# A fused attention-and-feed-forward kernel: a new written-out order on every engine, found with re-set transfer costs

## The chip, the cores and the metric

The kernel runs on one core of one Trainium2 chip. The core has a matrix engine (TensorE, PE in the profile, with its weight loads shown as PEld), three engines for elementwise work (VectorE is DVE, ScalarE is ACT, GpSimd is POOL) and SyncE (SP), which here issues nearly all DMA transfers. Every engine runs its own list of instructions strictly in order and waits at semaphores for what others have made. The metric is the device time of one execution in microseconds (us).

## The reference

```
phi(x)  = outer product of (S1 x) and (S2 x), 8 by 8 = 64 features    # x: 32 numbers per token and head
q_p, k_p = phi(q), phi(k)                  # q, k, v: 4 batches, 4 heads, 1088 tokens, 32 numbers
kv  = sum over tokens of k_p v             # 64 x 32 per batch and head
z   = sum over tokens of k_p
attn = (q_p kv) / (q_p z + 1e-6)
x   = attn with the heads side by side     # 4352 tokens of 128 numbers
h   = x @ w_in                             # 128 -> 2048
out = (h - tanh(h)) @ w_out                # 2048 -> 128, float32
```

## The kernel before

**Two halves that overlap.** The attention of a batch yields 1088 columns of `xT` (tokens along the free axis). The feed-forward walks over `xT` in ten windows (`layers`): two of 256 tokens, seven of 512, one of 256. A window `w` has sixteen first products `L1.w.j` (line 912, `w_in` times `xT` into a PSUM bank pair), tanh over up to four of them at once on ACT (line 916), and sixteen second products `L2.w.j` (line 925) that add up in bank 0. The term `h @ w_out` is done as one product with `w_in @ w_out`, which the kernel computes once: `turn0..3` transposes `w_in` on TensorE (line 857), `w_inT0..3` copies it (ACT, line 862), `wfold` multiplies (line 869), and `lin.w` (line 897) applies it. After the window, DVE copies bank 0 out (`osb`, line 931) and SP stores it (line 938).

**Attention of a batch b.** DVE transposes the loaded keys (`kT`, lines 569 and 573), TensorE projects (`kproj`, 582), DVE turns them (`kab`, 590), a small chain gives the weights for the denominator (`gram` 598, `zm` 603, `ufold` 606, `uw` 609). POOL and DVE form key products (`wk`, 629), and TensorE sums them with the values (`tiles` 642 for batch 0, `sums` 711 for the others; both need all four pieces of that batch's `v`). Queries: `qT` (739), `qproj` (751), `qab` (759), a divide chain (`dm` 778, `den`, `rden`, `qa` 787), query products `qp` (661 or 797), a transpose (`qt0` 676 with the copy `qpB` 683, or `qpT` 803), and the numerator `num` (693 or 820), whose result is copied into `xT` (`x`, 699, 830, 835). For batches 1 to 3 this stands between feed-forward products. Batch 0 has nothing to stand between: it is the opening, and the feed-forward starts behind it.

**What sets the order.** Each operation is recorded by `Program.op` with its engine, a cost and what it reads and writes. `schedule` places them. The list `ORDER` names for each engine the operations by number in the order in which they are to run; with it, the costs, rates and lags in the code no longer choose any order. What they still set is where TensorE's filler products (lines 503, 512 columns wide, and 504, 128 wide: products of zeros that keep the array busy in the opening) are put, because the scheduler fills the gaps that it computes. `sync` then derives every semaphore wait from the recorded dependences.

**Loads.** All go through SP's queue in the order of `ORDER["sync"]`: keys (`load_keys`, `load_rows`), queries (`load_rows`), values in four pieces per batch (`load_v`), `w_in` in four pieces `wi0..3` (`load_w_in`), `w_out` in four pieces `wo0..3` (`load_w_out`). `gated` adds a wait for an earlier load so that no more than about 2.4 MB are asked for ahead; the loads of batch 2 also wait for `x0.8` (the last copy of batch 0's numerators, DVE) and those of batch 3 for `x81.0` (the same of batch 1, ACT). SP waits at the instruction, so everything behind it in the queue waits as well. `w_in` and `w_out` are float32 in memory and are cast on chip: `cast_in0`, `cast_in1` on ACT, `cast_in2`, `cast_in3` and `cast_out0..3` on POOL (lines 843 and 847).

The one dependence that is touched is that of `psk0` and `psk1`, two small scaled copies on ACT (line 530), and the small operation `warm` (line 505, a tanh of one column, made ahead of need), which writes the tile `spare`.

Of the kernel before, what the change touches and what calls it, by code (L numbers as in the profile page):

```python
# [26 lines left out]
SEEN = {"tensor": 60, "scalar": 40, "vector": 50, "gpsimd": 70, "sync": 60}  # L27
MODE = 93
ISSUE = 460
BEGIN = 750  # L30
# [5 lines left out]

ORDER = {
    "tensor": (
# [14 lines left out]
    ),  # L53
    "scalar": (
# [4 lines left out]
    ),  # L59
    "vector": (  # L60
# [5 lines left out]
    ),  # L66
    "gpsimd": (
        "6 4 5 2 16 20 3 25 7 18 17 19 23 22 79 21 80 24 81 109 106 110 107 108 111 150 152 241 242 247 251 363 365 364 374 370 "
        "508 506 507 517 513 "
    ),  # L70
    "sync": (
# [3 lines left out]
    ),  # L75
}

# [16 lines left out]
class Program:  # L94
# [46 lines left out]
    def schedule(self):  # L141
# [7 lines left out]
            for x, i in enumerate(text.split()):  # L149
                turn[self.ops[int(i)]] = x  # L150
        head = dict.fromkeys(engines, 0)
        free = {e: 0 if e == "sync" else BEGIN for e in engines}
        avail = {e: [] for e in engines}
        for i, o in enumerate(self.ops):
            o.idx = i
# [7 lines left out]
        while left:  # L163
            best = None
            for e in engines:
# [4 lines left out]
                if turn:  # L170
                    o = min(avail[e], key=turn.get)
# [48 lines left out]
            order[e].append(o)  # L220
            left -= 1
            for k in o.kids:
                seen = o.end + SEEN[k.eng]
                if k.eng == e and not dma:
                    seen = o.at + o.cost if e == "tensor" else o.end
                k.ready = max(k.ready, seen)
                k.need -= 1
                if not k.need:
                    avail[k.eng].append(k)
# [114 lines left out]
def bass_polysketch_attn__then__act_tanh_shrink_kernel(nc, q, k, v, S1, S2, moe_w_in, moe_w_out, out):  # L344
# [92 lines left out]
    def load_small():  # L437
        for i, src in enumerate((S1, S2)):
            o = load("scalar", 1024, ("s_raw",), "s", -1000, lambda e, i=i, src=src: e.dma_start(
                out=s_raw[8 * i:8 * i + 8, :], in_=src[:, :]), True)  # L440
            o.lag = -950

    def cells(name, i, lo, hi):
        return [(name, i, c) for c in range(lo // 64, hi // 64)]
# [1 line left out]
    def load_rows(dst, src, name, b, cuts, prios, first=0):  # L446
        i = b % 2
        for x, (lo, hi) in enumerate(cuts):
            hi = min(hi, S)
            size = 512 * (hi - lo)  # L450
            o = P.op("sync", size / (360 if b else 280), lambda e, lo=lo, hi=hi: e.dma_start(
                out=dst[i][:, lo:hi], in_=src[b].rearrange("h (j c) d -> (h j) (c d)", j=32)[:, lo:hi]),
                w=cells(name + "raw", i, lo, hi), sem=f"{name}{i}{x + first}", prio=prios[x], name=f"load {name}{b}{x + first}",
                after=gated(size))
            o.lag = 2500 if b == 1 else 0 if b or first else 1100
            asked.append((o, size))

    def load_keys(prio):

        src = k[0].rearrange("h (j c) d -> (h j) (c d)", j=32)  # L460
        dst = kraw[0][:, :].rearrange("p (g f) -> p g f", f=KG)

        def runs(g0, g1, lo, hi):
            rows = src[:, KG * g0 + lo:KG * g0 + hi]
            rows = bass.AP(tensor=rows.tensor, offset=rows.offset, ap=[rows.ap[0], [KG, g1 - g0], rows.ap[1]])
            return lambda e: e.dma_start(out=dst[:, g0:g1, lo:hi], in_=rows)  # L466

        for x, (g0, g1, lo, hi) in enumerate(((0, 4, 0, 160), (0, 3, 160, 288), (3, 4, 160, 224))):
            size = 512 * (g1 - g0) * (hi - lo)
            o = load("sync", size, ("kraw0", min(x, 1)), f"k0{min(x, 1)}", prio, runs(g0, g1, lo, hi), x == 2, 280)  # L470
            if x == 2:
                asked.append((o, size))

    def load_v(b, prio):
        i = b % 2
        src = v[b].rearrange("h (j c) d -> j h c d", j=32)
        for g in range(4):
            n = 9 if g < 3 else 7
            o = load("sync", 128 * 128 * n, ("vx", i), f"v{i}", prio, lambda e, g=g, n=n: e.dma_start(  # L479
                out=vx[i][32 * g:32 * g + 32, :, 0:n, :].rearrange("j h t d -> j h (t d)"),  # L480
                in_=src[:, :, 9 * g:9 * g + n, :].rearrange("j h t d -> j h (t d)")), True, 230)
            o.lag = 2500 if b == 1 else 0 if b else 900
        asked.append((o, 128 * 128 * 34))

    def load_w_in(prio):
        for x in range(4):
            o = load("sync", 262144, ("w_in_f", x), f"wi{x}", prio, rate=390, fn=lambda e, x=x: e.dma_start(
                out=w_in_f[:, 512 * x:512 * x + 512], in_=moe_w_in[:, 512 * x:512 * x + 512]))

    def load_w_out(prio):  # L490
        for x in range(4):
            load("sync", 262144, ("w_out_f", x), f"wo{x}", prio, rate=300, fn=lambda e, x=x: e.dma_start(
                out=w_out_f[:, 4 * x:4 * x + 4, :],
                in_=moe_w_out[512 * x:512 * x + 512, :].rearrange("(jb ji) c -> ji jb c", jb=4)))

# [36 lines left out]
    def sketch():  # L532
# [7 lines left out]
        P.op("tensor", 100, put, r=[("s_raw",), ("ident",)], w=[bank[5]], prio=-3000, mode="32x32", name="psk", ni=16)  # L540
        for h in range(2):
            scaled(psk[:, :, h, :], ps[:, 5, 0:16].rearrange("p (a i) -> p a i", a=2), hmask[:, h:h + 1], 16,
                   [bank[5], ("hmask",)], [("psk", h)], -899.5, f"psk{h}")
        for i in range(2):
            P.op("scalar", act(16), lambda e, i=i: e.copy(w4[i][:, 0:16], ps[:, 5, 0:16]), r=[bank[5]], w=[("w4s", i)], prio=-880 + i, name=f"w4{i}")

# [518 lines left out]
```

## Time and profile before

| | |
|---|---|
| three executions | 108.99, 109.08, 109.91 us; median 109.08 |
| profiled execution | 108.55 us |
| its span (first to last instruction) | 106.7 us |
| TensorE matmul busy | 96.8 us, 91% |
| ACT busy | 78.4 us, 73% |
| DVE busy | 61.7 us, 58% |
| POOL busy | 35.0 us, 33% |
| moved by DMA | 11.21 MB |
| granted TensorE clock | 1.0 |

Some 1.85 us of the execution lie outside the span. The table's TensorE row holds everything the engine did, the filler products too. An engine's share over the whole span mixes the opening, in which engines wait for loads and for one another, with the long rest, in which feed-forward and attention overlap; the two have to be read apart. In the timeline a row of several matmuls has the time from the first one's start to the last one's end, the end of its pipeline included, so that rows overlap a little; in the chain the same row has only the step to the next.

### The profile page before, as it was taken

The page shows a single profiled execution, that of the slowest core. Times are in us where ns is not written, and L with a number is a line of the kernel's source. Part 1 is how long each engine was busy: PE and PEld are TensorE (multiplying, and loading weights), DVE is VectorE, ACT ScalarE, POOL GpSimd, SP SyncE. Part 2 cuts the span into 40 slices and gives each one's busy share as a digit, 9 for nine tenths or more (in the row PEclk, how much of TensorE's full clock was granted, in tenths as well). Part 3 has the DMA queues.
Part 4 walks back from the last instruction along what each step waited for, and adds up shares of the span by engine and source line. Part 5 has one row for each costly group of instructions (what it writes and reads, how often), then busy time and mean ns, then how long its engine had stood idle before and what let it go on. Part 6 is the DMA issues. An engine that isn't in the chain of part 4 may idle for free.

```text
span 106.7 us, 2954 instructions
## 1 busy us (share of the span) xinstructions
PE 96.8 (91%) x1246; PEld 50.5 (47%) x1256; DVE 61.7 (58%) x128; ACT 78.4 (73%) x107; POOL 35.0 (33%) x45
## 2 busy tenths in 40 slices
PE   6899985899999969999899999999999999999960
PEld 3357553784656424424544443544344434345540
DVE  2467962999899998689986365927650020200210
ACT  3350874775458974859998797989969999999930
POOL 5737017450491920493930049391000000000000
PEclk9999999999999999999999999999999999999999
DMA  2999999930798300799100410033002324024063
GB/s 38 298 220 289 313 320 259 238 82 0 247 201 233 57 3 0 242 208 262 25 0 7 75 22 0 6 52 47 0 12 37 55 34 68 0 36 62 6 98 49
DMA packets 26509, 11.21 MB, mean 105 GB/s; under 512 B 19072, under 2 KB 24320, under 8 KB 26496
## 3 DMA queue, kind: packets, MB, share of 16 engines
q1 hardware_dynamic: 25920, 10.95, 43.7%
q8 instruction: 10, 0.16, 0.7%
q10 hardware_dynamic: 576, 0.07, 0.4%
q14 instruction: 3, 0.02, 0.1%
HBM read 8.78 MB, written 2.23 MB: 103 GB/s over the span
## 4 chain that ended last, share of the span: by engine, by line
PE 64%; DMA 10%; DVE 9%; ACT 4%; POOL 4%; SPq 3%; issue 3%; POOLq 0%; DVEq 0%
PE ps L925 23%; PE ps L912 23%; DMA w_out_f<-in_moe_w_out_dram 6%; ACT tt L916 4%; DMA vx<-in_v_dram 4%; PE ps L820 4%; PE ps L897 3%; DVE qpT L803 3%; POOL w_out L847 2%; PE ps L751 2%; DVE qp L797 2%; PE ps L582 2%; DVE qab L759 1%; SPq L466 1%; SPq L479 1%
## 5 line engine op out<-in xcount | busy, mean ns | idle before, releaser
L916 ACT ACTIVATE tt<-ps 128x1024 bf16<-128x1024 f32 (+1 forms) x70 | 66.7, 998 | 10.4 <-PE ps L912 8.5
L912 PE MATMUL ps<-xT,w_in 128*128 128x512 bf16 (+1 forms) x154 | 40.9, 346 | 1.6 <-issue 0.8
L925 PE MATMUL ps<-tt,w_out 128*128 128x512 bf16 (+1 forms) x157 | 39.9, 347 | 0.2 <-issue 0.2
L629 POOL TENSOR_TENSOR wk<-kab 128x768 f32<-128x768 f32 (+2 forms) x11 | 15.7, 1425 | 22.3 <-DVE kab L590 21.8
L925 PEld LDWEIGHTS ps<-tt,w_out 128*128 128x128 bf16 x160 | 15.4, 99 | 13.9 <-issue 2.2
L912 PEld LDWEIGHTS ps<-xT,w_in 128*128 128x128 bf16 x160 | 14.3, 97 | 16.0 <-ACT tt L916 4.9
L931 DVE STREAM_TRANSPOSE osb<-ps 128x512 f32<-128x512 f32 (+1 forms) x10 | 6.3, 634 | 22.6 <-PE ps L925 22.6
L797 POOL TENSOR_TENSOR qp<-qa,qab 128x768 f32<-128x768 f32 x6 | 10.3, 1710 | 6.2 <-DVE qa L787 5.9
L803 DVE STREAM_TRANSPOSE qpT<-qp 128x768 f32<-128x768 f32 x9 | 8.4, 959 | 3.1 <-POOL qp L797 3.1
L759 DVE STREAM_TRANSPOSE qab<-ps 128x576 f32<-128x576 f32 (+2 forms) x10 | 6.0, 642 | 3.7 <-PE ps L751 3.7
L739 DVE STREAM_TRANSPOSE qT<-qraw 128x576 f32<-128x576 f32 (+2 forms) x9 | 5.8, 653 | 0.0
L820 PE MATMUL ps<-qpT,kvw 32*32 32x288 f32 (+1 forms) x192 | 4.6, 399 | 0.8 <-DVE qpT L803 0.8
L503 PE MATMUL ps<-wz 128*128 128x512 bf16 x8 | 4.3, 583 | 1.0 <-DVE hmask L513 1.0
L590 DVE STREAM_TRANSPOSE kab<-ps 128x576 f32<-128x576 f32 (+2 forms) x5 | 3.2, 661 | 2.1 <-PE ps L582 2.1
L569 DVE STREAM_TRANSPOSE kT<-kraw 128x576 f32<-128x576 f32 x6 | 4.4, 751 | 0.0
L847 POOL CAST w_out<-w_out_f 128x512 bf16<-128x512 f32 x4 | 2.5, 615 | 5.6 <-DMA w_out_f<-in_moe_w_out_dram 5.2
L830 ACT CAST xT<-ps 128x256 bf16<-128x256 f32 x6 | 2.0, 377 | 3.0 <-PE ps L820 3.0
L797 DVE TENSOR_TENSOR qp<-qa,qab 128x768 f32<-128x768 f32 x3 | 4.2, 1411 | 0.0
L862 ACT COPY w_inT<-ps 128x512 bf16<-128x512 bf16 x4 | 2.3, 586 | 2.3 <-PE ps L857 2.2
L820 PEld LDWEIGHTS ps<-qpT,kvw 32*32 32x32 f32 x192 | 2.4, 103 | 2.8 <-DVE qpT L803 1.2
L711 PEld LDWEIGHTS ps<-wk,vx 128*32 128x32 f32 x216 | 3.2, 110 | 1.2 <-issue 1.2
L843 ACT CAST w_in<-w_in_f 128x512 bf16<-128x512 f32 x2 | 1.2, 618 | 3.3 <-DMA w_in_f<-in_moe_w_in_dram 3.3
(90 smaller groups left out, 94.5 us busy)
## 6 DMA issues: line engine op xcount, KB each, us to landing
vx<-in_v_dram SPq DMA_DIRECT2D x12, 144.0 KB, 4.0
qraw<-in_q_dram SPq DMA_DIRECT2D x4, 288.0 KB, 6.2
w_in_f<-in_moe_w_in_dram SPq DMA_DIRECT2D x4, 256.0 KB, 5.5
w_out_f<-in_moe_w_out_dram SPq DMA_DIRECT2D x4, 256.0 KB, 6.7
out_dram<-osb SPq DMA_DIRECT2D x16, 64.0 KB, 2.0
kraw<-in_k_dram SPq DMA_DIRECT2D x3, 288.0 KB, 5.5
kraw<-in_k_dram SPq DMA_DIRECT2D x3, 256.0 KB, 5.9
qraw<-in_q_dram SPq DMA_DIRECT2D x3, 256.0 KB, 5.5
```

What stands on the lines that cost most here:

```text
L569: P.op("vector", dve(hi - lo), lambda e, lo=lo, hi=hi: e.transpose(out=kT[:, lo:hi], in_=kraw[i][:, lo:hi]), r=cells("kraw", i, lo, min(hi ...
L629: P.op(eng, dve(cols) if eng == "vector" else pool2(cols), lambda e, t0=t0, t1=t1, ap=ap, m=m, ka0=ka0: e.tensor_tensor(out=wk[:, t0:t1, : ...
L739: P.op("vector", dve(hi - lo), lambda e: e.transpose(out=qT[i][:, lo:hi], in_=qraw[i][:, lo:hi]), r=cells("qraw", i, lo, hi), w=cells("qT" ...
L759: P.op("vector", dve(2 * n), lambda e, h=h: e.transpose(out=qab[:, t0:t1, h:h + 2, :].rearrange("p t h x -> p h t x"), in_=ps[:, qb + h:qb ...
L797: P.op(eng, dve(cols) if eng == "vector" else pool2(cols), lambda e, p0=p0, p1=p1, w=w: e.tensor_tensor(out=qp[:, p0:p1, :, :, :].rearrang ...
L803: P.op("vector", dve(cols), lambda e, p0=p0, p1=p1: e.transpose(out=qpT[:, p0:p1, :, :, :].rearrange("p t h y j -> p (t h y j)"), in_=qp[: ...
L820: ins = e.matmul(ps[32 * h:32 * h + 32, nb[g], 0:32 * n], kvw[i][32 * g:32 * g + 32, y, 32 * h:32 * h + 32], qpT[32 * g:32 * g + 32, t0:t0 ...
L847: P.op("gpsimd", 600, lambda e, x=x: e.tensor_copy(w_out[:, 4 * x:4 * x + 4, :], w_out_f[:, 4 * x:4 * x + 4, :]), r=[("w_out_f", x)], w=[( ...
L912: P.op("tensor", pe(n), lambda e, jb=jb + y, y=y, hb=hb: e.matmul(hb[:, n * y:n * y + n], w_in[:, 128 * jb:128 * jb + 128], xT[:, f0:f0 + ...
L916: P.op("scalar", act(q * n), lambda e, un=un, hb=hb, q=q: e.activation(out=tt[:, un, 0:q * n], in_=hb[:, 0:q * n], func=AF.Tanh, scale=-1. ...
L925: P.op("tensor", pe(n), lambda e, jb=jb, un=un, y=y: e.matmul(acc[:, 0:n], w_out[:, jb, :], tt[:, un, n * y:n * y + n], start=(not f0 and ...
L931: P.op("vector", dve(n), lambda e: e.transpose(out=osb[u][:, 0:n], in_=acc[:, 0:n]), r=[ka], w=[("osb", u)], prio=slot0, name=f"osb{w}")
```

## The change

Four of the five lists of `ORDER` stand in another order throughout (TensorE, ACT, DVE, POOL), and SP's, the order in which loads and stores are issued, from its tenth entry on. The operations are the same, with the same shapes. The rates and lags in `load_small`, `load_rows`, `load_keys`, `load_v`, `load_w_in` and `load_w_out`, the scheduler's starting time for SP, and the time at which POOL sees a load are given other values. `psk0` and `psk1` now also read `spare`, so they stand behind `warm`. The filler products change with the costs: 9 wide and 15 narrow ones stand where 8 and 18 stood.

What the numbers in `ORDER` mean, for the places that the prediction speaks of (names as above; a dot stands for what is left out):

```
SP, before:    ... v0 (4 pieces) wi0 wi1 wi2 wi3 q02 wo0 wo1 wo2 wo3 k10 k11 v1 (4 pieces) q10 q11 | k20 k21 v0 v0 v0 v0 q20 q21 out0 x4 out1 x4 | k30 k31 v1 x4 q30 q31 out2 x4 ...
SP, after:     ... v0 (4 pieces) wi0 wi3 wi1 wi2 wo2 q02 wo1 wo0 wo3 k11 v1 v1 v1 k10 q10 q11 | v0 k21 v1(the fourth piece of batch 1) k20 q21 out0 out0 out1 out0 q20 v0 | q30 out1 v1 out0 v1 v0 k30 v1 out1 v0 k31 out1 out2 v1 q31 ...
ACT, before:   s s psk1 psk0 warm mask s2blk2 w41 s2blk1 w40 s2blk0 s2blk3 ka0 cast_in1 kvs0 cast_in0 kvb0 kvb1 qpB0.1 qpB0.0 x0.1 w_inT0 w_inT1 x0.0 w_inT2 tanh.0.0 w_inT3 tanh.0.4 tanh.0.2 tanh.0.12 tanh.0.8 ...
ACT, after:    s s warm psk0 psk1 mask s2blk1 w41 s2blk3 ka0 s2blk2 w40 s2blk0 kvs0 cast_in0 kvb0 kvb1 qpB0.1 qpB0.0 cast_in1 w_inT0 x0.0 w_inT1 x0.1 w_inT2 tanh.0.0 tanh.0.2 w_inT3 tanh.0.4 tanh.0.8 tanh.0.12 ...
POOL, before:  ... wk0.0 (memset) wk0.2 (memset) wk0.4 cast_out1 cast_in2 cast_out2 cast_in3 cast_out0 cast_out3 qp0.5 ...
POOL, after:   ... wk0.0 wk0.2 wk0.4 cast_out2 cast_in2 (memset vx) (memset qT) cast_in3 (memset kraw) cast_out1 cast_out0 cast_out3 qp0.5 ...
PE, before:    ... psk f f s2p kproj0.0 ... num0.1 turn0 qt0.2 turn1 num0.0 num0.2 turn2 L1.0.0 L1.0.6 L1.0.1 qproj0.4 turn3 (seven L1.0) wfold L1.0.14 L1.0.12 L2.0.0 ...
PE, after:     ... psk F s2p kproj0.0 ... num0.1 turn0 qt0.2 num0.0 turn1 num0.2 turn2 L1.0.0 L1.0.1 L1.0.2 qproj0.4 L1.0.3 L1.0.6 turn3 (seven L1.0) L2.0.0 .. L2.0.3 wfold L2.0.4 ...
               (F is a wide filler, f a narrow one)
```

```diff
 ORDER = {
...
     "sync": (
-        "28 29 30 31 32 33 34 35 36 37 38 39 40 41 42 43 44 45 46 47 48 49 50 51 52 53 253 254 255 256 257 258 259 260 212 213 "
...
+        "28 29 30 31 32 33 34 35 36 37 40 38 39 44 41 43 42 45 47 48 49 50 46 52 53 255 254 51 253 260 212 213 285 214 259 256 "
...
-        free = {e: 0 if e == "sync" else BEGIN for e in engines}
+        free = {e: BEGIN for e in engines}
...
-                seen = o.end + SEEN[k.eng]
+                seen = o.end + SEEN[k.eng] + (300 if dma and k.eng == "gpsimd" else 0)
...
-            o.lag = -950
+            o.lag = 500 * i - 500
...
-            o = P.op("sync", size / (360 if b else 280), lambda e, lo=lo, hi=hi: e.dma_start(
+            o = P.op("sync", size / (340 if b else 290), lambda e, lo=lo, hi=hi: e.dma_start(
...
-            o.lag = 2500 if b == 1 else 0 if b or first else 1100
+            o.lag = 1500 if b == 1 else 300
...
-                in_=src[:, :, 9 * g:9 * g + n, :].rearrange("j h t d -> j h (t d)")), True, 230)
-            o.lag = 2500 if b == 1 else 0 if b else 900
+                in_=src[:, :, 9 * g:9 * g + n, :].rearrange("j h t d -> j h (t d)")), True, 190 if b == 0 else 240)
+            o.lag = 1500 if b == 1 else 0 if b else 300
...
-            o = load("sync", 262144, ("w_in_f", x), f"wi{x}", prio, rate=390, fn=lambda e, x=x: e.dma_start(
+            o = load("sync", 262144, ("w_in_f", x), f"wi{x}", prio, rate=300, fn=lambda e, x=x: e.dma_start(
...
-            load("sync", 262144, ("w_out_f", x), f"wo{x}", prio, rate=300, fn=lambda e, x=x: e.dma_start(
+            load("sync", 262144, ("w_out_f", x), f"wo{x}", prio, rate=290, fn=lambda e, x=x: e.dma_start(
...
-                   [bank[5], ("hmask",)], [("psk", h)], -899.5, f"psk{h}")
+                   [bank[5], ("hmask",), ("spare",)], [("psk", h)], -899.5, f"psk{h}")
```

More of the change, by code (lines that the diff above doesn't have):

```diff
@@ L54 @@
     "scalar": (
[4 rows of a table removed]
[4 rows of a table added]
     ),
     "vector": (
[5 rows of a table removed]
[5 rows of a table added]
     ),
     "gpsimd": (
-        "6 4 5 2 16 20 3 25 7 18 17 19 23 22 79 21 80 24 81 109 106 110 107 108 111 150 152 241 242 247 251 363 365 364 374 370 "
-        "508 506 507 517 513 "
+        "24 16 2 3 4 19 5 25 6 20 7 17 18 79 80 81 110 106 22 23 107 21 109 108 111 150 152 241 242 247 251 363 365 364 370 374 "
+        "506 508 507 517 513 "
     ),
     "sync": (
[3 rows of a table removed]
[3 rows of a table added]
     ),
@@ L469, in load_keys @@
             size = 512 * (g1 - g0) * (hi - lo)
-            o = load("sync", size, ("kraw0", min(x, 1)), f"k0{min(x, 1)}", prio, runs(g0, g1, lo, hi), x == 2, 280)
+            o = load("sync", size, ("kraw0", min(x, 1)), f"k0{min(x, 1)}", prio, runs(g0, g1, lo, hi), x == 2, (350, 378, 100)[x])
+            o.lag = -200
             if x == 2:
```

48 rows, old and new, of the table ORDER are left out of this document.

## The prediction

> **What bounds the kernel now.** I read the page's busy shares first, then the busy time by stretches, then the chain that ended last, and only then the timeline of the opening.
>
> ```profile
> PE 96.8 (91%) x1246; PEld 50.5 (47%) x1256; DVE 61.7 (58%) x128; ACT 78.4 (73%) x107; POOL 35.0 (33%) x45
> ...
> 15.00:20.00 5.00, 3.42 (x63) 2.02 (x62) 3.00 (x6) 2.96 (x6) 3.69 (x6) 1.00 1.10 265
> ...
> 20.00:103.00 83.00, 80.37 (x972) 40.79 (x982) 49.20 (x87) 68.73 (x81) 24.72 (x16) 1.00 0.34 73
> ```
>
> In the stretches the columns are the window, its length, then PE, PEld, DVE, ACT and POOL busy. From 20 us on TensorE works 80.37 of 83.00 us at the full granted clock (1.00): 2.63 us is all that a better order could win there. From 15 to 20 us it stands still for 1.58 us. No edit removes or shrinks an operation of the feed-forward, so the time is the moment at which TensorE's dense work begins, plus that work, plus its stalls.
>
> ```profile
> 9.45 6.01 DMA w_out_f<-in_moe_w_out_dram
> ...
> 15.51 0.62 POOL w_out L847
> ...
> 16.28 0.62 POOL w_in L843
> ...
> 19.27 0.63 POOL w_out L847
> ...
> 19.99 1.05 PE ps L869 x16
> ```
>
> This is the chain (start, length, what). A piece of `w_out` (`wo1`) lands at 15.46, and six casts follow one another on POOL, (19.27 - 15.51) / 5 = 0.75 us from start to start, up to `wfold` at 19.99. `cast_in2` and `cast_in3`, whose data came earlier, stand second and fourth behind it.
>
> ```profile
> 17.04 0.38 PE L857 MATMUL ps<-identb,w_in 128*128 128x128 bf16 x4 [0.99 <-POOL w_in L843]
> 17.26 0.49 PE L912 MATMUL ps<-xT,w_in 128*128 128x256 bf16 x3
> 17.68 0.55 PE L751 MATMUL ps<-qT,w 32*32 32x160 f32 x32
> ...
> 39.78 1.55 PE L820 MATMUL ps<-qpT,kvw 32*32 32x288 f32 x64 [0.81 <-DVE qpT L803]
> ```
>
> So `turn2` waits 0.99 us for `cast_in2`, and the first feed-forward product `L1.0.0`, behind it on TensorE, runs at 17.26. The one large stall later is 0.81 us before `num1.0`, where DVE's chain from the queries of batch 1 ends.
>
> **The change, part by part.**
>
> *POOL and the order of `w_out`.* When does `wo2`, now first, land?
>
> ```profile
> L487 SPq DMA_DIRECT2D w_in_f<-in_moe_w_in_dram x4: 430/432/432, 5.2 to 6.6; - x4
> ...
> DMA to landing us min/median/max: 5.0/5.5/6.3
> ```
>
> The last piece of `w_in` is issued at 6.6 and lands at most 6.3 later, 12.9. From there to 15.46 came `q02` (288 KB), `wo0` and `wo1` (256 KB each): 800 KB in 2.56 us, or 0.82 us for a `w_out` piece. `wo2` now stands right behind `w_in`, so in the order of issue it lands at 12.9 + 0.82 = 13.7, though it is issued late:
>
> ```profile
> 9.45 0.93 SPq L492 DMA_DIRECT2D w_out_f<-in_moe_w_out_dram  x2
> ...
> DMA to landing us min/median/max: 6.0/6.7/7.0
> ```
>
> Its wait (for the values of batch 0, met before at 9.45) now holds SP from 7.0 to 9.45, with `q02` queued behind; the megabyte of `w_in` in flight until 12.9 keeps the transfers busy meanwhile. These rows are the other bound: 6.0 to 7.0 from issue would be 15.45 to 16.45. I take 13.7, since the 6 to 7 us were waits behind other bytes, and keep the others as a rival.
> Then `cast_out2` runs 13.75 to 14.4 and `cast_in2` until 15.1. Three memsets now stand among the casts:
>
> ```profile
> L524 POOL MEMSET vx<- 32x256 f32 x2 | 0.6, 307 | 0.1
> L523 POOL MEMSET kraw<- 128x64 f32 x2 | 0.3, 153 | 0.1
> L525 POOL MEMSET qT<- 128x64 f32 x2 | 0.3, 152 | 0.1
> ```
>
> They add 0.31 + 0.15 + 0.15 and three gaps of 0.75 - 0.62 = 0.13, some 1.0 us, yet the last cast ends at 13.75 + 6 × 0.75 + 1.0 = 19.25 where it ended at 19.9. The other three `w_out` pieces (15.5, 16.3, 17.1 by the same spacing) come before their turns (16.7, 17.5, 18.2). `wfold`, moved behind four second products, is then not late. `q02` comes at 14.6; its transpose on DVE stands behind work that ends after 15.2:
>
> ```profile
> 15.26 0.77 DVE L739 STREAM_TRANSPOSE qT<-qraw 128x576 f32<-128x576 f32 x1
> ```
>
> *The psk copies behind `warm`.*
>
> ```profile
> 1.82 1.28 ACT L530 ACT_TABLE_LOAD   x1 [1.82 <-DVE hmask L515]
> 4.75 0.44 ACT L530 ACTIVATE psk<-ps,hmask 128x16 f32<-128x16 f32 x2 [1.64 <-PE ps L535]
> 5.08 0.20 ACT L505 ACTIVATE spare<-wz 128x1 f32<-128x1 bf16 x1
> ```
>
> The copies wait for TensorE until 4.75; table load and `warm` (1.28 + 0.20) fit before that from any start up to 3.2. Nothing, either way; without the cover, 1.5 us.
>
> *Fillers.*
>
> ```profile
> 2.44 1.46 PE L503 MATMUL ps<-wz 128*128 128x512 bf16 x3
> ...
> 4.62 0.39 PE L504 MATMUL ps<-wz 128*128 128x128 bf16 x2
> 4.95 0.63 PE L551 MATMUL ps<-s_raw,e 16*128 16x32 f32 x2
> ```
>
> Between `psk` and `s2p` one wide filler (a third of 1.46, 0.49) takes the place of two narrow ones (0.39; 0.33 to the next instruction). `s2p`, `kproj0.0` and the chain behind them come 0.1 to 0.2 us later; I take +0.2. The fillers left out later stand in waits for other engines: nothing.
>
> *ACT's order.*
>
> ```profile
> 10.92 0.62 ACT L843 CAST w_in<-w_in_f 128x512 bf16<-128x512 f32 x1 [3.34 <-DMA w_in_f<-in_moe_w_in_dram]
> 11.45 0.26 ACT L648 COPY kvs<-ps 128x128 f32<-128x128 f32 x1
> ...
> 12.98 0.77 ACT L683 COPY qpB<-ps 128x256 f32<-128x256 f32 x2 [0.18 <-PE ps L676]
> ...
> 15.29 0.59 ACT L862 COPY w_inT<-ps 128x512 bf16<-128x512 bf16 x1 [0.49 <-PE ps L857]
> 15.77 0.27 ACT L699 CAST xT<-ps 128x128 bf16<-128x128 f32 x1
> ```
>
> `kvs0` no longer stands behind the cast; I count no gain, since the products it reads come 0.2 later by the filler. From the `qpB` pair (12.98 + 0.2, until 13.95) ACT does `cast_in1` (0.62: 14.57), `w_inT0` (0.59: 15.16), `x0.0` (0.27: 15.45). `turn1` waits for `w_inT0` and takes 0.38, like `turn2` above (15.6), so `w_inT1` runs until 16.25 and `x0.1` until 16.5. `turn2` (0.22 to the next instruction, 17.04 to 17.26 above) follows `w_inT1` at 16.3, 1.2 us after `cast_in2`. `L1.0.0` follows at 16.7, bound by `x0.1`: **0.55 us ahead** of 17.26.
>
> *The stages behind it.* `qproj0.4` needs three products first instead of being fourth: 17.05 against 17.68, a lead of 0.6 that DVE's chain inherits.
>
> ```profile
> 18.43 0.91 DVE L759 STREAM_TRANSPOSE qab<-ps 128x320 f32<-128x320 f32 x2 [1.90 <-PE ps L751]
> ...
> 30.88 1.45 DVE L759 STREAM_TRANSPOSE qab<-ps 128x576 f32<-128x576 f32 x2 [0.23 <-PE ps L751]
> ...
> 53.65 0.43 PE ps L925 x2
> ```
>
> DVE has the same operations up to `num1.0` (`whi` earlier, `qT10` and `qT11` exchanged, `kvw1` one place later), so `num1.0` keeps that lead, and the 0.81 us wait before it stays, bounded by nothing and 0.9. TensorE has one 512-column product less done there (`L2.2.7` moves behind): 0.43 / 2 = 0.2 given back if nothing idle takes it up. Later swaps are of neighbours, or, like `fold3` and `x83.0`, sit beside idle DVE or ACT; I cost them at nothing, with 0.4 both ways.
> Sum: between 0.6 - 0.2 and 0.6, so 0.55 us less: profiled 108.55 - 0.55 = 108.0; the median lies 0.53 above that execution, so **108.5 us**.
>
> *SP's later order.*
>
> ```profile
> DMA to landing us min/median/max: 3.6/4.3/6.7
> ...
> 26.08 0.80 SPq L451 DMA_DIRECT2D kraw<-in_k_dram  x2
> ...
> 32.80 1.21 PE L711 MATMUL ps<-wk,vx 128*32 128x64 f32 x72
> ...
> 42.18 0.84 SPq L451 DMA_DIRECT2D kraw<-in_k_dram  x2
> 43.06 2.77 SPq L479 DMA_DIRECT2D vx<-in_v_dram  x4
> ...
> 51.47 1.21 PE L711 MATMUL ps<-wk,vx 128*32 128x64 f32 x72
> ```
>
> The fourth `v` piece of batch 1 now stands third behind the wait for `x0.8` (26.08 before, some 25.4 after): issued at 26.3, landed at 29.9 to 33.0, wanted by `sums1` at about 32.5. The last `v` piece of batch 2 stands tenth behind the wait for `x81.0` (42.18 before, 41.4 after, as it is also one place earlier on ACT): behind four `v` pieces at 0.69 (2.77 / 4) and five others at 0.42 (0.84 / 2) it is issued at 46.3 and landed at 49.9 to 53.0, wanted by `sums2` at 50.9. By the median landings (30.6, 50.6) neither stops TensorE, the second by a hair.
> The Trainium skill ("DMA: Bandwidth & Descriptors", "Anatomy of one DMA — SWDGE (gpsimd) path") gives 2.0 us and the bytes at 436 GB/s for a transfer by itself on the other issue path; for 114 KB that is an estimate of 2.3, by which no piece is late and the sum stays. The shortest landing here, 3.6, is longer, so the rows decide.
>
> **The rivals.**
> *The first cast waits for its load (slower).* POOL now begins with `wo2`, and `cast_in2`, `turn2`, `L1.0.0` queue behind: `L1.0.0` = landing + 0.05 + 0.75 + 0.62 + 0.3. It decides from a landing of 15.0; above 15.5 the gain is gone. If the transfers in flight share the bandwidth, `wo2` lands with the batch, up to 17.1, and `L1.0.0` runs at 18.8, 1.55 late: 110.6. With 6.0 to 7.0 from issue it is 17.2 to 18.2: 109.0 to 110.0. Against it speak the 0.7 to 0.9 us steps in which the pieces landed. The Trainium skill (same page, "Queues, rings and completion order") says that completion on one issuing engine's queue is not in order of issue; this trace shows steps in order, but no case with 128-byte runs behind it.
> *A `v` piece is late (slower).* With the longest landing, 6.7, `sums2` waits 2.1 us, less 0.55 won: 110.6. For it: stores now stand between the pieces. Against: the median suffices.
> *The lead is lost on DVE (no change).* If `q02` lands after 15.6, or POOL's casts slow DVE beside them, `num1.0` is no earlier: 109.1.
> *More is won (faster).* Half of the 0.81 wait and a third of the other stalls (2.63 - 0.81 = 1.8 us) go as well, 0.55 + 0.4 + 0.6: 107.5.
>
> **How the numbers follow.** The forecast has 0.47, more won 0.18, no change 0.15, the late cast 0.14, the late `v` piece 0.06. The range from 107.4 to 110.1 leaves out the late piece, half of the late cast and part of what is more than expected. One per cent, 1.09 us, is about what a measurement here can tell from no change. Faster than that: more won and the edge of the forecast, 0.20; slower: the late piece and the worse part of the late cast, with part of an unseen stall, 0.15; the same 0.65.
>
> **What would show it.** The first POOL cast of line 847 near 13.8 and `L1.0.0` near 16.7; no wait of line 857 for POOL; the chain of waits enters TensorE's work through ACT (`x0.1`) rather than through the `w_out` load; some 0.7 to 0.9 us idle before line 820 near 39; line 711 without a DMA ahead of it. Wrong it is if that cast starts after 15, if line 711 waits for `vx`, or if TensorE's busy time from 20 us on falls below 96.8%.

## The result and the profile after

The changed kernel takes **108.02 us** (median of 8 runs, 107.41 to 108.59) against 109.01 for the kernel before, measured beside it (8 runs, 108.40 to 109.91): a ratio of **0.990**, with a 95% interval of 0.986 to 0.994. That is 0.99 us less, where 0.55 was forecast. Here and below, ratios and their intervals leave out executions more than 1.5% above the fastest of the same kernel. The profiled execution took 107.41 us with a span of 105.6 (before 108.55 and 106.7), so what lies outside the span is as it was, and 1.1 us are to be found inside.

The page's busy shares and two stretches of the changed kernel, then a stretch of the kernel before (the columns are those of the prediction's stretches):

```profile
PE 97.0 (92%) x1243; PEld 50.2 (48%) x1254; DVE 60.4 (57%) x128; ACT 78.5 (74%) x107; POOL 35.9 (34%) x45
...
15.00:20.00 5.00, 4.86 (x78) 2.95 (x77) 3.89 (x10) 4.57 (x9) 3.74 (x9) 1.00 1.04 291
...
20.00:102.00 82.00, 78.90 (x957) 39.41 (x965) 46.98 (x83) 67.48 (x79) 25.57 (x16) 1.00 0.32 70
```

```profile
20.00:102.00 82.00, 79.37 (x965) 40.20 (x976) 49.20 (x87) 68.18 (x81) 24.72 (x16) 1.00 0.33 72
```

From 15 to 20 us TensorE now works 4.86 of 5.00 us, where it was 3.42: 1.44 us won. From 20 us on it works 0.47 us less than before in the same 82 us: part of what was won is given back later. Two places show how. The first is the opening; the chain of the changed kernel, then its timeline:

```profile
9.25 4.83 DMA w_out_f<-in_moe_w_out_dram
...
14.13 0.62 POOL w_out L848
...
14.90 0.62 POOL w_in L844
...
41.57 3.38 DMA out_dram<-osb
...
44.97 0.73 DVE osb L932
```

```profile
13.00 0.77 ACT L684 COPY qpB<-ps 128x256 f32<-128x256 f32 x2 [0.43 <-PE ps L677]
13.67 0.62 ACT L844 CAST w_in<-w_in_f 128x512 bf16<-128x512 f32 x1
...
15.05 0.27 ACT L700 CAST xT<-ps 128x128 bf16<-128x128 f32 x1 [0.24 <-PE ps L694]
...
15.37 0.58 ACT L863 COPY w_inT<-ps 128x512 bf16<-128x512 bf16 x1
...
15.86 0.27 ACT L700 CAST xT<-ps 128x128 bf16<-128x128 f32 x1
...
16.01 0.23 PEld L858 LDWEIGHTS ps<-identb,w_in 128*128 128x128 bf16 x4 [0.39 <-ACT w_inT L863]
...
16.25 0.49 PE L913 MATMUL ps<-xT,w_in 128*128 128x256 bf16 x3
...
18.36 0.35 DVE L779 TENSOR_TENSOR dm<-qab 128x160 f32<-128x160 f32 x1
...
19.33 0.90 PEld L870 LDWEIGHTS ps<-w_out,w_inT 128*128 128x128 bf16 x16 [0.34 <-POOL w_out L848]
...
38.08 1.55 PE L821 MATMUL ps<-qpT,kvw 32*32 32x288 f32 x64 [0.80 <-DVE qpT L804]
...
44.97 0.72 DVE L932 STREAM_TRANSPOSE osb<-ps 128x512 f32<-128x512 f32 x1 [1.09 <-DMA out_dram<-osb]
...
45.75 0.39 PE L898 MATMUL ps<-xT,whi 128*128 128x512 bf16 x1 [0.43 <-DVE osb L932]
...
50.28 1.21 PE L712 MATMUL ps<-wk,vx 128*32 128x64 f32 x72
```

The first `w_out` piece lands 4.83 us after its issue at 9.25, and POOL's first cast begins at 14.13 where it was 15.51. `cast_in2` follows at 14.90 (16.28 before), and `turn2` at 16.01 no longer waits for POOL: its weight load waits for `w_inT1` on ACT. `L1.0.0` runs at 16.25, 1.01 us ahead. At `num1.0` the lead is 39.78 - 38.08 = 1.70.

The second place is where the chain runs through a store, with the rows near 45 us of the timeline. The result copy of window 2 (`osb`, at 44.97) needs a buffer that window 0's last store still reads; that store goes out only at 41.57 and takes 3.38 us. DVE waits 1.09 us for it, and the product `lin.3`, which needs the bank that DVE empties, waits another 0.43. The same two rows of before, the second and third here, had no such wait; the first is `dm0.4` of before, which is needed further down:

```profile
19.37 0.69 DVE L778 TENSOR_TENSOR dm<-qab 128x160 f32<-128x160 f32 x1
...
45.88 0.72 DVE L931 STREAM_TRANSPOSE osb<-ps 128x512 f32<-128x512 f32 x1 [0.31 <-PE ps L925]
...
46.97 0.38 PE L897 MATMUL ps<-xT,whi 128*128 128x512 bf16 x1
```

The lead shrinks from 1.70 to 51.47 - 50.28 = 1.19 at `sums2` and is 1.06 at the last result copy (103.12 before, 102.06 after). SyncE's own waits (in all, times, longest) and its timeline show why the store is late:

```profile
SPq L451 <- ACT xT L831: 5.1, 1, 5.1
```

```profile
40.21 0.35 SPq L451 DMA_DIRECT2D qraw<-in_q_dram  x1
...
40.60 0.43 SPq L939 DMA_DIRECT2D out_dram<-osb  x1
41.07 0.45 SPq L480 DMA_DIRECT2D vx<-in_v_dram  x1
41.57 0.43 SPq L939 DMA_DIRECT2D out_dram<-osb  x1
```

The store of 41.57 stands third behind a load of the queries of batch 3 (40.21). That load waits 5.1 us for `x81.0`, a copy of the result of `num1.0`, and the last piece of window 0's output, which has nothing to do with it, waits too.

### The profile page after: what moved, and what is told of

Its sections match the earlier page's. It is cut to its first block, busy times and chain, and to the rows that moved or that the text cites. A ratio compares the mean times of both kernels' runs of the same rounds, so it can differ in the third digit from the quotient of the medians.

```text
span 105.6 us, 2945 instructions
## 1 busy us (share of the span) xinstructions
PE 97.0 (92%) x1243; PEld 50.2 (48%) x1254; DVE 60.4 (57%) x128; ACT 78.5 (74%) x107; POOL 35.9 (34%) x45
## 4 chain that ended last, share of the span: by engine, by line
PE 58%; DMA 12%; DVE 10%; ACT 5%; SPq 4%; POOL 4%; issue 3%; POOLq 0%; DVEq 0%
PE ps L926 21%; PE ps L913 21%; DMA w_out_f<-in_moe_w_out_dram 5%; ACT tt L917 5%; PE ps L821 4%; DMA vx<-in_v_dram 4%; PE ps L898 4%; DMA out_dram<-osb 3%; DVE qpT L804 3%; POOL w_out L848 2%; DVE qp L798 2%; DVE osb L932 2%; SPq L480 2%; PE ps L752 1%; DVE qab L760 1%
## 5 line engine op out<-in xcount | busy, mean ns | idle before, releaser
L913 PE MATMUL ps<-xT,w_in 128*128 128x512 bf16 (+1 forms) x151 | 40.4, 346 | 1.3 <-issue 0.6
L798 POOL TENSOR_TENSOR qp<-qa,qab 128x768 f32<-128x768 f32 x6 | 11.2, 1867 | 7.3 <-DVE qa L788 7.1
L898 PE MATMUL ps<-xT,whi 128*128 128x512 bf16 (+1 forms) x10 | 3.5, 353 | 0.7 <-DVE osb L932 0.4
L712 PE MATMUL ps<-wk,vx 128*32 128x64 f32 x216 | 3.6, 220 | 0.0
```

Of the source, the lines that this page charges most:

```text
L712: ins = e.matmul(ps[32 * h:32 * h + 32, vb, 0:64], vx[i][:, h, t, :], wk[:, t, h, :, :], start=(t == 0), stop=(t == NT - 1), tile_position ...
L798: P.op(eng, dve(cols) if eng == "vector" else pool2(cols), lambda e, p0=p0, p1=p1, w=w: e.tensor_tensor(out=qp[:, p0:p1, :, :, :].rearrang ...
L898: P.op("tensor", pe(n), lambda e, x=x: e.matmul(acc[:, 0:n], x[:, :], xT[:, f0:f0 + n], start=f0 > 0 and x is whi, stop=not f0 and x is wl ...
L913: P.op("tensor", pe(n), lambda e, jb=jb + y, y=y, hb=hb: e.matmul(hb[:, n * y:n * y + n], w_in[:, 128 * jb:128 * jb + 128], xT[:, f0:f0 + ...
```

## The experiments

The experiments' times lie apart by up to 1.5 us already where the first loads land, so they are read by stages too. Starts in us of `turn0`, `L1.0.0`, `num1.0` and the last result copy, and the three stretches between them:

| kernel | `turn0` | `L1.0.0` | `num1.0` | last copy | to `L1.0.0` | to `num1.0` | to the end |
|---|---|---|---|---|---|---|---|
| before | 13.78 | 17.26 | 39.78 | 103.12 | 3.48 | 22.52 | 63.34 |
| after | 13.80 | 16.25 | 38.08 | 102.06 | 2.45 | 21.83 | 63.98 |
| after, old loads | 13.36 | 19.74 | 43.71 | 108.34 | 6.38 | 23.97 | 64.63 |
| the same, 13 fillers | 14.28 | 19.72 | 41.44 | 106.09 | 5.44 | 21.72 | 64.65 |
| the same, 6 fillers | 13.93 | 18.25 | 40.46 | 104.69 | 4.32 | 22.21 | 64.23 |
| before, new loads | 14.88 | 18.02 | 40.59 | 103.95 | 3.14 | 22.57 | 63.36 |
| before, `w_in` casts first | 13.70 | 16.44 | 38.59 | 101.87 | 2.74 | 22.15 | 63.28 |
| after, early store | 13.49 | 15.95 | 37.94 | 101.51 | 2.46 | 21.99 | 63.57 |
| after, early store, `w_in` casts first | 14.30 | 16.75 | 38.69 | 102.26 | 2.45 | 21.94 | 63.57 |

### The old order of loads in the changed kernel

```diff
 SP, opening:
-... wi0 wi3 wi1 wi2 wo2 q02 wo1 wo0 wo3 k11 v1 v1 v1 k10 q10 q11 | v0 k21 v1 k20 ...
+... wi0 wi1 wi2 wi3 q02 wo0 wo1 wo2 wo3 k10 k11 v1 v1 v1 v1 q10 q11 | v0 k21 k20 ...
```

> The changed kernel with the opening's loads issued in the old order (q02 wo0 wo1 wo2 wo3, then k10 k11 and all of v1); POOL still casts wo2 first. Theory (POOL's first cast waits for its load, everything behind it on POOL, TensorE and ACT queues up): wo2 lands near 16.3 us of the span instead of 14.1, cast_in2 ends near 17.8, turn2 and the first feed-forward product run near 18.0 instead of 16.25, so all of the 1.0 us lead at that product and 0.7 us more are lost; at the end of the span 1.0 to 1.8 us later than the changed kernel, ratio to the kernel before 1.00 to 1.01. Rival (the lead comes from the orders of ACT, DVE and TensorE and the loads hardly matter): the first product still runs before 16.8 and the ratio stays at 0.99.

Measured: 111.53 us, ratio 1.021 (1.013 to 1.029). The profiled execution, 113.69 us, is the longest of its five. Its timeline and its clock row:

```profile
17.84 0.61 POOL L849 CAST w_out<-w_out_f 128x512 bf16<-128x512 f32 x1 [7.99 <-DMA w_out_f<-in_moe_w_out_dram]
...
19.36 0.58 PE L859 MATMUL ps<-identb,w_in 128*128 128x128 bf16 x4 [2.97 <-POOL w_in L845]
19.74 0.85 PE L914 MATMUL ps<-xT,w_in 128*128 128x256 bf16 x3
...
PEclk9999998559999999999999999999999999999998
```

`wo2`, third of the four in the old order, lands at 17.8 instead of 14.1, and the `w_in` cast and `turn2` queue behind its cast. So POOL's new order needs the new order of loads; the direction is as expected, but the loss is some 1 us larger. In this execution the piece lands 1.5 us later than the expected 16.3, and the granted clock falls to about half in the stand of 2.97 us, so that three products take 0.85 us where they take 0.49.

### The same with TensorE kept busy ahead of `turn2`

```diff
             for o in order[e]:
+                if o.name == "turn2":
+                    for _ in range(13):      # 6 in the second kernel
+                        self.keep(eng)       # a 512-column product of zeros into bank 4
```

> The changed kernel with the old load order of the opening, as in the run whose first product came at 19.7 us after TensorE had stood for 2.97 us, with thirteen wide products of zeros (2.8 us) put into that stand ahead of turn2; they write a bank that nothing holds then and change no result. Theory (the long stand costs twice: the late load itself and then a lower granted clock for some 5 us): the clock row stays at 9 throughout, the first feed-forward products run at 0.11 us each instead of 0.2, and the end comes 1 to 2 us earlier than with the old loads alone; ratio 1.004 to 1.012 instead of 1.021. Rival (the late load alone makes the loss): the clock returns but the end moves by less than 0.3 us, ratio 1.018 to 1.022.

With 13 the ratio is 1.022 (1.017 to 1.026). The clock row holds at 9, but the fillers run until 19.5:

```profile
16.68 2.98 PE L1040 MATMUL ps<-wz 128*128 128x512 bf16 x13
19.49 0.39 PE L862 MATMUL ps<-identb,w_in 128*128 128x128 bf16 x4
```

In that execution `cast_in2` had ended at 18.19, so the fillers themselves held `turn2` back. This run doesn't separate the price of the clock. The second kernel has 6:

> The kernel after with the old order of loads in the opening, as before, but with 6 wide products of zeros (0.22 us each, some 1.3 us) ahead of turn2 instead of 13 (2.98 us, which themselves held turn2 back by 1.2 us). They break the stand of 2.97 us into one of at most 1.7. If the stand's length lowered the clock: the clock row stays at 9 throughout, turn2 follows the cast of cast_in2 by no more than 0.1 us, the three first products take 0.49 instead of 0.85, and the time lies between the 1.00 to 1.01 first expected of the old loads and 1.021, near 1.012 (some 1 us less than 111.5). If the old loads cost their 1.02 by the late landing alone, the ratio stays at 1.02 with the clock at 9.

Measured: ratio 1.0125 (1.005 to 1.020), 110.48 us.

```profile
16.51 0.61 POOL L852 CAST w_out<-w_out_f 128x512 bf16<-128x512 f32 x1 [6.63 <-DMA w_out_f<-in_moe_w_out_dram]
...
18.03 0.38 PE L862 MATMUL ps<-identb,w_in 128*128 128x128 bf16 x4 [0.24 <-POOL w_in L848]
18.25 0.49 PE L917 MATMUL ps<-xT,w_in 128*128 128x256 bf16 x3
...
PEclk9999999999999999999999999999999999999999
```

`turn2` now follows its cast after 0.15 us (17.88 to 18.03) and the clock stays up. From `L1.0.0` to `num1.0`, where both kernels do the same work, the one with the halved clock takes 23.97 us and this one 22.21: the halved clock cost some 1.76 us in that execution. It does not explain the ratio of 1.021, though: the three executions behind that ratio took 111.36, 111.50 and 111.53 us at mean granted clocks of 0.984, 0.999 and 0.984, so the one whose clock stayed up was no shorter. The medians of the two kernels differ by 1.05 us, their intervals overlap, and here the piece had landed 1.3 us earlier; what makes up that difference stays open. Most of what is lost here is the late landing: the stretch to `L1.0.0` is 1.87 us longer than in the changed kernel, of 2.59 us between the two profiled executions (110.00 and 107.41 us).

### The new order of loads in the kernel before

```diff
 SP, opening:
-... wi0 wi1 wi2 wi3 q02 wo0 wo1 wo2 wo3 k10 k11 v1 (4 pieces) q10 q11 | ...
+... wi0 wi3 wi1 wi2 wo2 q02 wo1 wo0 wo3 k11 v1 v1 v1 k10 q10 q11 v1 | ...
```

> The kernel before with the opening's loads in the new order (wi0 wi3 wi1 wi2 wo2 q02 wo1 wo0 wo3 k11 v1 k10, with all of v1 before batch 2) and nothing else: POOL still casts wo1 first, which is now the third of the five transfers as it was before. Theory (load order and cast order only work as a pair): the first cast still starts near 15.5, the first feed-forward product near 17.3, ratio 0.998 to 1.003. Rival (the loads by themselves bring the lead): the first product before 16.9, ratio 0.992 or less.

Measured: 108.94 us, ratio 0.996 (0.993 to 0.9996).

```profile
17.78 0.40 PE L858 MATMUL ps<-identb,w_in 128*128 128x128 bf16 x4 [0.62 <-POOL w_in L844]
```

`turn2` still waits for POOL, 0.62 us instead of 0.99: POOL's first cast here is that of `wo1`, now second in the queue of `w_out`. The stage to `L1.0.0` shrinks by 0.34 us, a third of the change's 1.03. This execution's opening is late as a whole, with `turn0` at 14.88 instead of 13.78, so its first product (18.02) misses the expected 17.3. The changed kernel without the new loads gives 1.021, the kernel before with them alone 0.996; the whole change gives 0.990.

### The two `w_in` casts first, in the kernel before

```diff
 POOL:
-... wk0.4 cast_out1 cast_in2 cast_out2 cast_in3 cast_out0 cast_out3 ...
+... wk0.4 cast_in2 cast_in3 cast_out1 cast_out2 cast_out0 cast_out3 ...
```

> The kernel before with one edit: on POOL the two casts of w_in stand ahead of the four casts of w_out; loads and all other orders are the old ones. Theory (the old kernel's late start is cast_in2 standing behind a w_out load): turn2 no longer waits for POOL, the first feed-forward product runs at 16.1 to 16.4 us instead of 17.26, but the last w_out cast still ends no earlier than 17.2 + 0.75 = 18.0 to 19.2; the end comes 0.4 to 1.0 us earlier than before, ratio 0.991 to 0.996. Rival (the search's many small swaps make the gain): within 0.2 us of before, ratio 0.998 to 1.002.

Measured: 107.63 us, ratio 0.985 (0.978 to 0.992).

```profile
12.84 0.62 POOL L844 CAST w_in<-w_in_f 128x512 bf16<-128x512 f32 x1 [0.46 <-DMA w_in_f<-in_moe_w_in_dram]
...
15.68 0.62 POOL L848 CAST w_out<-w_out_f 128x512 bf16<-128x512 f32 x1 [2.22 <-DMA w_out_f<-in_moe_w_out_dram]
...
16.44 0.49 PE L913 MATMUL ps<-xT,w_in 128*128 128x256 bf16 x3
...
18.55 0.32 DVE L779 TENSOR_TENSOR dm<-qab 128x160 f32<-128x160 f32 x1
```

Both casts are done before the first `w_out` piece lands, and two entries moved in one list gain at least as much as the whole change. The loads may then stay as they were: the stall was the order on POOL, not the bytes. The gain is larger than expected (0.991 to 0.996). The stretch to `L1.0.0` is 0.74 us shorter than before, and the next one 0.37, the size of `dm0.4`, which takes 0.32 us where it took 0.69. To the end, 63.28 us, this kernel also has nothing of the loss behind `num1.0`.

### Window 0's last store ahead of the loads

```diff
 SP:
-... k20 q21 out0 out0 out1 out0 q20 v0 | q30 out1 v1 out0 v1 ...
+... k20 q21 out0 out0 out1 out0 out0 q20 v0 | q30 out1 v1 v1 ...
```

> The changed kernel with the last store of the first output window (out0) issued right behind its third, instead of behind loads of batches 2 and 3. Theory (the copy osb2 into that output buffer waits 1.09 us for that store to land at 44.97, and the first product of window 3's linear term waits 0.43 us on TensorE behind it, which loses some 0.5 us of lead): osb2 no longer waits, line 898 runs near 45.2 instead of 45.75, and the end comes 0.3 to 0.6 us earlier than in the changed kernel; ratio 0.985. Rival (ACT, which is busy without a break behind that place, sets the pace there anyway): the wait goes and the end moves by less than 0.15 us.

Measured: 107.24 us, ratio 0.983 (0.977 to 0.989), the lowest of all.

```profile
44.05 0.72 DVE L933 STREAM_TRANSPOSE osb<-ps 128x512 f32<-128x512 f32 x1 [0.31 <-PE ps L927]
...
45.01 0.38 PE L899 MATMUL ps<-xT,whi 128*128 128x512 bf16 x1
```

The copy waits for its product alone and `lin.3` for nothing; from `num1.0` to the end it takes 63.57 us instead of 63.98. Of the 0.64 us that the change had lost there, one store moved by five places gives back 0.41.

### The wait ahead of `num1.0`

```diff
 PE:
-... num1.0 L2.2.7 L2.2.8 L2.2.9 ...
+... L2.2.7 L2.2.8 L2.2.9 num1.0 ...
```

> The changed kernel with three second products of window 2 (L2.2.7 to L2.2.9, 0.65 us in all) moved on TensorE from behind the numerators of batch 1 to ahead of them. Theory (TensorE waits 0.80 us there for DVE, and work that is ready can fill it): the wait before line 821 near 38 shrinks from 0.80 to 0.1 to 0.2, and if TensorE sets the rest of the time the end comes 0.5 to 0.65 us earlier, ratio 0.984. Rival (ACT sets the pace from 46 to 52, where its five tanh follow one another without a gap): the wait is filled but the time comes back as waits for tanh or for osb2 before 52, the end moves by less than 0.2 us, ratio 0.989.

Measured: 107.71 us, ratio 0.987 (0.982 to 0.993), its last copy at 102.06 as in the changed kernel.

```profile
38.36 1.55 PE L822 MATMUL ps<-qpT,kvw 32*32 32x288 f32 x64
...
40.43 0.39 PE L914 MATMUL ps<-xT,w_in 128*128 128x512 bf16 x1 [0.52 <-ACT xT L832]
```

The 0.80 us wait is gone, and 0.52 of it stands one place later: the products moved ahead were the work that covered the copies of `num1.0`'s result. This run alone doesn't decide, because `lin.3` runs at 45.74 as in the changed kernel (45.75), held by the same late store. A second kernel adds the early store and fills the new hole with `L2.2.10` and `L2.2.11`.

> The changed kernel with out0's last store early (as in the run before that did only this) and, on TensorE, L2.2.7 to L2.2.9 ahead of num1.0 and L2.2.10, L2.2.11 directly behind it, ahead of L1.2.13. Theory (the wait before num1.0 is time that could be filled, but what stood behind num1.0 covered ACT's copies of its result, so other ready work has to take that place): the wait before line 820 falls to 0.1 to 0.3 us, L1.2.13 waits at most 0.1 us for ACT, and the end comes 0.3 to 0.5 us earlier than with the store alone; ratio to the kernel before 0.978 to 0.981. Rival (ACT sets the pace from 46 us on): the end as with the store alone, ratio 0.983, with TensorE's waits for tanh grown by what was filled.

It gives 107.35 us and 0.984 (0.981 to 0.987), no different from the early store alone, though `num1.0` no longer waits. Moving these products gained nothing with the store out of the way either; that DVE and ACT pace this stretch fits the waits, but was not shown by a run that makes one of them faster.

### The early store, with `whi` back in its old place

```diff
 DVE:
-... qp0.4 whi qp0.6 kT11 qp0.8 qpB0.4 qpB0.6 qpB0.8 ...
+... qp0.4 qp0.6 kT11 qp0.8 qpB0.4 qpB0.6 whi qpB0.8 ...
```

> The changed kernel with out0's last store early and the small copy whi on DVE put back behind qpB0.6, where it stood before the change. Theory (whi between qp0.4 and qp0.6 lets qp0.6 run apart from POOL's product: 0.41 us where it took 0.85 before the change, and this is most of the lead that grew from 1.0 at the first product to 1.7 us at num1.0): qp0.6 takes about 0.85 again, num1.0 comes 0.3 to 0.45 us later than with the store alone (near 38.3 where that one has 37.94), and the end 0.2 to 0.4 us later; ratio 0.986. Rival (the lead grew through other places, and the order of whi only exchanges work): num1.0 within 0.1 us, ratio 0.983.

Measured: 107.47 us, ratio 0.985 (0.981 to 0.989). From `turn0` to `num1.0` it takes 24.37 us, against 24.45 with the early store alone, whose `dm0.4` took 0.51 us instead of 0.33 here, and 24.28 in the changed kernel, whose `dm0.4` took 0.35. DVE's earlier `whi` explains some 0.1 us of the lead, where 0.3 to 0.45 was expected.

### The early store and the `w_in` casts first

```diff
 POOL (SP as in the early store):
-... wk0.4 cast_out2 cast_in2 (memset vx) (memset qT) cast_in3 (memset kraw) cast_out1 ...
+... wk0.4 cast_in2 cast_in3 cast_out2 (memset vx) (memset qT) (memset kraw) cast_out1 ...
```

> The kernel after with out0's last store directly behind its third (0.983 alone) and POOL's two w_in casts ahead of its first w_out cast, in the new order of loads. If the opening only needs that cast_in2 doesn't wait for a w_out piece that lands late: the casts of w_in run at some 12.5 to 13.5 (they wait for the last w_in piece), turn2 still follows w_inT1 on ACT at some 16.0, L1.0.0 at some 16.25, and the ratio stays at 0.98 to 0.985 (the w_out casts end up to 0.3 us earlier, which wfold may show). If w_out's place on POOL in itself matters (an earlier start of the whole chain), 0.97 to 0.98 and L1.0.0 before 16.0.

Measured: 107.77 us, ratio 0.987 (0.982 to 0.992).

```profile
16.51 0.23 PEld L859 LDWEIGHTS ps<-identb,w_in 128*128 128x128 bf16 x4 [0.39 <-ACT w_inT L864]
...
18.86 0.54 DVE L780 TENSOR_TENSOR dm<-qab 128x160 f32<-128x160 f32 x1
```

The casts of `w_in` now run from 11.81 to 13.16 and that changes nothing: `turn2` waits 0.39 us for ACT as before, and `L1.0.0` comes 2.45 us after `turn0`, exactly as in the changed kernel. The ratio lies just above the expected 0.98 to 0.985, which its interval covers. Once POOL is out of the way, ACT's copies are the bound.

## Why the prediction was right in direction and too small

**Right.** The gain was to come from the wait of `turn2` for POOL, and it does: that wait is gone, ACT ends last ahead of `turn2`, and each run that brings the wait back loses the gain. The first cast was predicted at 13.75 and came at 14.13, not behind the rival's landing of 15.45 to 16.45, and the last one ended at 18.66 + 0.62 = 19.28 (19.25 predicted). The cover of `psk` held: table load at 1.70, `warm` at 3.00, the copies at 4.73 as before. The 0.81 us ahead of `num1.0` stayed at 0.80. No `v` piece is late: `sums2`, quoted above, runs without a wait. The rival's sum for a late landing holds too: with six fillers the piece lands at 16.46, which gives 16.46 + 0.05 + 0.75 + 0.62 + 0.3 = 18.18 for `L1.0.0`, and 18.25 was measured.

**Right by luck: the landing.** The prediction had the last piece of `w_in` land at 12.9 and `wo2` 0.82 us behind it. In the changed kernel the last of these loads is issued at 6.6 and lands at most 5.2 us later:

```profile
L488 SPq DMA_DIRECT2D w_in_f<-in_moe_w_in_dram x4: 430/432/433, 5.2 to 6.6; - x4
...
DMA to landing us min/median/max: 4.5/4.8/5.2
```

That is 11.8, and `wo2` lands 2.3 us behind it, at 9.25 + 4.83 = 14.08. One term was 1.1 us too late and the other 1.5 too short, and they nearly cancel; what sets the 2.3 us wasn't tested.

**Mis-sized: the opening, 0.55 for 1.01.** Two terms. The filler was priced at +0.2; it was +0.10 at `kproj0.0` (5.51 to 5.61) and 0.02 at the first `qproj` (9.48 to 9.50), since the fillers just ahead of it took 0.60 us (8.90 to 9.50) where they took 0.68 (8.80 to 9.48). And the ACT sum added whole recorded durations and the products between them, and had `x0.1` end at 16.5. In the rows above each instruction starts a little before the recorded end of the one ahead (`cast_in1`, 0.62 long, is followed after 0.56, `w_inT1`, 0.58 long, after 0.49), so `x0.1` ends at 15.86 + 0.27 = 16.13, and `L1.0.0` follows at 16.25 instead of 16.7.

**Wrong: that DVE's chain only inherits the lead.** It grew from 1.02 at `qab0.4` (18.43 before, 17.41 after) to 1.70. Half of the growth is one row: `dm0.4` (19.37 in the row of before) took 0.69 us with a POOL cast beside all but the end of it (19.27 to 19.89), and takes 0.35 in the changed kernel's profile, where the cast that runs when it begins ends at 18.53 and the next starts at 18.66. The prediction had POOL's casts as a rival that slows DVE; here they slowed it less than before. The other runs agree: 0.72 us with six fillers, where the cast beside it runs from 20.30 to 20.91 and `dm0.4` starts at 20.36, 0.54 with a cast beside two thirds of it, 0.32 in the kernel before with the `w_in` casts first. But the 0.35 is in part luck. The kernels with the same orders on POOL and DVE up to this row took 0.33 us for it (early store, `whi` back), 0.51 (the early store alone) and 0.63 (each of the two that fill the wait), and `num1.0` came 24.37 to 24.56 us after `turn0` in them, against 24.28 in the changed kernel and 26.00 before. So up to 0.3 of the 1.70 belongs to that one execution. The other half, small gaps around `qpB0.4` and the key transposes, wasn't isolated; `whi` has some 0.1 us of it. The Trainium skill ("GPSIMD Engine Reference", "1. Specifications") says that GPSIMD shares its SBUF interfaces with VectorE and contends with DVE instructions that have two SBUF inputs; `dm`, a product of two SBUF tiles, fits that with 0.35 against 0.69 us.

**Missing: the store.** The step "SP's later order" followed the `v` pieces alone and costed the rest at nothing. The rival of the late `v` piece named the stores that now stand between those loads as what could delay a load; that a load which waits could delay a store, and through the buffer the copy, the bank and a product, was not asked. It takes back 0.51 us of the lead between `num1.0` and `sums2`, and moving it recovers 0.41 to the end; the other 0.2 of the 0.64 weren't traced. The 0.2 that the prediction had TensorE give back behind `num1.0` for `L2.2.7` was not the cause up to there: with the early store, and that product in it, the stretch from `num1.0` to `sums2` takes 11.63 us, against 11.69 before.

**Wrong criteria.** The chain of waits was to enter through `x0.1`; it still enters through the load of `w_out` and POOL's casts, since `wfold`, which was to be not late, waits 0.34 us for the last cast (0.38 before) and runs at 19.33. That chain doesn't show what sets `L1.0.0`. And TensorE's busy share from 20 us on fell from 96.8 to 78.90 / 82.00 = 96.2%: by the prediction's own mark the part behind the opening was wrong, and it was, by the store.

In sum: 0.46 us too little in the opening, 0.69 missed on DVE, and 0.64 lost unforeseen behind `num1.0`. The last two nearly cancel, which is luck, since neither was in the sum, and 0.5 us more than forecast is left. "More is won" was the rival nearest to it in size (107.5), but not in its mechanism: the wait that it took away stayed.

## What to carry to other kernels

On an in-order engine, look which work stands behind a wait that it doesn't need: two casts moved ahead of one that waits for a late load were worth 1.5% here (0.8 to 2.2), at least as much as the lists written anew. A queue that issues both loads and stores has to be read in both directions: a load held by a gate holds the stores behind it, and with them the buffers and banks that those stores would free. Before filling a wait, look whether the work to be moved there covers the next wait: here it did, and nothing was gained.

## What the runs showed of the hardware that was not expected

- In one execution TensorE stood for 2.97 us, from 16.40 to 19.36. The granted clock was 1.00 until 18.5, averaged 0.69 from 18.5 to 19.0, was 0.50 from 19.0 to 25.5 and then came back: it fell some 2.3 us after the last product, stayed down for some 6.8 us and cost some 1.76 us. The Trainium skill ("TensorE: Matmul & The Clock Gate", "Part 1: The HAM clock gate") gives about 3.4 us as the idle window after which the clock halves; here 2.97 us were enough. With six products of zeros in the stand, 1.47 us, it stayed up.
- The same 256 KB piece of `w_out` landed 4.83 us after its issue with only `w_in` still under way ahead of it, and 7.96 in the execution with `q02` and two more pieces ahead of it. How much of that is the bytes ahead wasn't measured by itself.
- `dm0.4`, an elementwise product of 128x160 on DVE, ended with POOL's cast. In eleven of the twelve profiled kernels a cast was running when it began, and in each it ended 0.16 to 0.20 us after that cast, whether it took 0.32 us in all or 0.75. In the twelfth (early store, `whi` back) none was running: it took 0.33 us, and the cast that began 0.08 us after it took 0.72 us instead of 0.61. So it did not run slower in proportion to the time beside each other; it looks as if each waited for the other to be done.
